# Head-mixing attention and two FFNs on one core: each batch's v load cut into eight DMAs, and a new listed order

## The chip, the core and the metric

The kernel runs on one core of a Trainium2 chip. The metric is the device time of one execution in microseconds (us). The profile tells the engines apart as PE (TensorE's matmuls), PEld (its weight loads), DVE (VectorE), ACT (ScalarE), POOL (GpSimd) and SP (SyncE, which issues most of the DMAs here). "Clock" is the share of TensorE's full speed that was granted in a stretch.

## The reference, cut to what matters

```python
def _attn_ref(q, k, v, w_pre, w_post):           # 4 batches, 12 heads, 448 rows, 64 columns
    scores = matmul(q, k^T) / sqrt(64)
    scores = einsum('bhij,hg->bgij', scores, w_pre)      # heads mixed before the softmax
    attn = softmax(scores)                               # over j
    attn = einsum('bhij,hg->bgij', attn, w_post)         # heads mixed after it
    return matmul(attn, v)

x = attn_out as (1792, 768)
x = (sigmoid(x @ w_gate) * (x @ w_val)) @ w_out          # 768 -> 1536 -> 768
h = x @ w_in                                             # 768 -> 2048
out = (h * sigmoid(1.702 * h)) @ w_out2                  # 2048 -> 768
```

All data are float32.

## The kernel before

The program has an attention part (the first 400 us) and the two feed-forward networks behind it, which this change leaves as they are.

In the attention a batch is cut into four units of 120 or 88 rows of q. For each unit PE first makes the scores of six pairs of heads (`qk`, L340), and DVE or ACT copy them from PSUM to the tile `sc` (`qk_out`). The unit is then taken in groups. For a group, SP moves rows of `sc` into a tile `gt` with two DMAs (`relayout`, L359) so that heads lie along the partitions; PE mixes the heads (`premix`, L368); DVE takes the maximum, ACT the exponential; PE mixes again (`postmix`, L415); DVE or ACT copy the result to the tile `at`. When all groups of a unit are done, PE multiplies `at` with v (`av`, L436). There are five `gt` tiles. Between these steps the q and k of the next batch are loaded into tiles `nat` (L291), turned on PE (`turn`, L300) and split in two parts, and 28 weight blocks of the first FFN are loaded (`pf`, L932), converted and stored again (`kept`, L898).

The tile `vt` holds the v of one batch; there is one such tile, so that a batch's v can be loaded only when the last `av` of the batch before has read it. `load_v` (L326) does it with two DMAs: x = 0 brings four of seven row groups into partitions 0 to 63, x = 1 the other three into partitions 64 to 127, each for all twelve heads. The first `av` of a batch needs both.

All of this is cut into pieces (`Work.add`), each with the engines that may run it. The order of all pieces on all engines, the engine of each piece and its PSUM banks stand in a table of numbers, `PLAN`, which `Work.order` reads: a token is the number of a piece in base 36, a letter for an engine where there is a choice, and banks behind a colon. The due times and costs in the calls of `work.add` are not used when the program is built. Every engine runs its own list in this order and waits for other engines by semaphores, so SP issues its DMAs strictly one after the other.

Of the kernel before, what the change touches and what calls it, by code (L numbers as in the profile page):

```python
# [74 lines left out]
0Y 3:0 1S 6:1 7V 1cY cS 1f:2 f:3 1oY 8 oS pS dY 4V 5 20:45 10S 11Y gV h r:6 sV 1gS 1h 1dS 1pS 2Y qY 21S u:7 vV  # L75
t i:1 eY jS k w 13:0 1r:3 16:2 14S 17V 22V 1i:6 1jS 23:41 1sS 1k 2c:75 15 25S 12S 24V 9:6 aS 18 2eS 1u:1 29:04
1t 1vV 1w 2dS 2bS 26:23 28S 1qY 2f:51 2aV 27V dd de 19:7 l:0 1x:4 2gS 2hV mV 1aV 1b b 4z:32 51V df:5 x:1 yV
1eS n dgV dh 1yS 1z 58:76 5aV 52:20 59S 54S 5e:75 2i 2j 2k:04 2l 53S 2v 50S di:2 2w 38 39 5gS 2n 3l 3m 3y 3z
4b 5fS z 2x:63 2y 2m 1l:5 1mV 1n 2z 2o 55:70 56S 4c 1fg 30 5b:15 5dV 3a:64 3b djS dk 31 32 2p 3c 3n:75 3d 3e
5cS 3f 2q 33 34 2r 57S 40:32 41 42 3o 3g 3h 3p 2s:64 3q 43 2tV 3r 3i:10 44 45 4d:37 4e 2uS 4g 4o 3jV 3kV 4f 4h  # L80
4i 4j 5h 7w:56 7yV 46 3s 5i 7xS 35:24 36S 3t 82:31 dl 7z:70 80V 37V 83S 84S 4k 88:56 89S 5u 85:23 87V 4l:17 3u
81V 3v:45 4mV 3wS 4nV 3xS 5j:30 47 48:17 5k 4p 5v 5m 86S 8b:45 49S 4aV 5l 5n 5w:21 4q:7 8cV 5x 5y 1fw 4r 67 68
5o 6k 5p 5q 8aV 4s dn:3 1fx 5z 60 69:40 4u:2 4v 6l 6x 6y 7a 7b 1fh 4w 8dV dt 5r:65 61 4tV 1fy 1fz 6a 8e 6b 6c
6d doS 6m:17 4xS dp 62 5sS 5tS 1g0 6z:40 7c:32 8f 8r 8s 6n 6p 6e 6o 6q 63 70 6f 71 72 73 1g2 at:65 avS auV
# [48 lines left out]
150:36 15d:71 15p 161 11rS 151 153 1jd 17cS 15e 122:05 123V 162 16e 124V 152 154 1jk 12f:24 12gS 12hS 1jj 14s
1jl 163:36 164 166 165 1jm 1jn 1jo 15q:05 14t 16f 17k 14u 15f 155 17l 156 1fs 15g 15r 17x 167 15t 157 12i:2
12j 12k 12m:4 12lS 12n 12o 12pV 15h 15i 16g:37 16h 15j 15s 15u 15k 16j 14v:62 16i 14wS 14xV 17m:10 17n 17y 18a
16k 17p 18b 158:45 15l:36 159V 15aV 17o 17q 16l 15mS 16m 168 169 16n 15v 19z:27 1ab:14 1adV 1a0S 16a 1acS
1a5:50 15nV 1a7V 1jq 1jr 1js 16o:32 16b:41 1jt 1ju 16cV 18c:60 1a6S 16pS 16r 1a1S 16dS 1a2:53 15w 1a3V 16qS
18n 1ae:71 18d 1agS 16s 18o 190 191 1a4S 1afV 18e 17r 1a8:42 1aaS 15x 1jp 18f 18g 1jw 15y:51 15zV 18p:37 18q
# [1635 lines left out]
```

## Time and profile before

| | |
|---|---|
| time, median of 3 runs | 1292.66 us (1284.29 to 1293.9) |
| profiled execution | 1287.18 us |
| its span | 1285.4 us |
| PE busy | 1247.9 us (97%) |
| DVE, ACT, POOL busy | 78%, 64%, 4% |

The span goes from the first to the last instruction of the profiled execution; the device time of the same execution lies 1.8 us above it. PE's busy time includes the time in which a matmul is only in flight, so 97% doesn't mean that PE works at its peak.

### The profile page before, as it was taken

The page shows a single profiled execution, that of the slowest core. Times are in us where ns is not written, and L with a number is a line of the kernel's source. Part 1 is how long each engine was busy: PE and PEld are TensorE (multiplying, and loading weights), DVE is VectorE, ACT ScalarE, POOL GpSimd, SP SyncE. Part 2 cuts the span into 40 slices and gives each one's busy share as a digit, 9 for nine tenths or more (in the row PEclk, how much of TensorE's full clock was granted, in tenths as well). Part 3 has the DMA queues.
Part 4 walks back from the last instruction along what each step waited for, and adds up shares of the span by engine and source line. Part 5 has one row for each costly group of instructions (what it writes and reads, how often), then busy time and mean ns, then how long its engine had stood idle before and what let it go on. Part 6 is the DMA issues. An engine that isn't in the chain of part 4 may idle for free.

```text
span 1285.4 us, 33205 instructions
## 1 busy us (share of the span) xinstructions
PE 1247.9 (97%) x12770; PEld 1115.6 (87%) x12770; DVE 1004.2 (78%) x2142; ACT 819.4 (64%) x1968; POOL 57.8 (4%) x138
## 2 busy tenths in 40 slices
PE   7999899899999999999999999999999999999998
PEld 5677676678679899989999999999999999999998
DVE  6787587698876999988889898878866795565863
ACT  3877587688884767667567666656665455565442
POOL 3111011010110000000000000000000000000000
PEclk9998899899999999999999999999999999999999
DMA  6877777677776665489976445894626872125653
GB/s 165 229 206 235 184 204 229 179 226 225 222 261 207 200 214 171 130 268 326 326 266 218 142 155 195 287 304 158 220 73 172 284 271 81 50 62 156 213 156 123
DMA packets 216111, 256.87 MB, mean 200 GB/s; under 512 B 60413, under 2 KB 202513, under 8 KB 215953
## 3 DMA queue, kind: packets, MB, share of 16 engines
q1 hardware_dynamic: 208944, 249.32, 61.7%
q0 software_dynamic: 1344, 4.05, 1.0%
q10 hardware_dynamic: 5664, 1.38, 0.5%
q8 instruction: 101, 1.65, 0.5%
q14 instruction: 58, 0.47, 0.1%
HBM read 160.18 MB, written 55.97 MB: 168 GB/s over the span
## 4 chain that ended last, share of the span: by engine, by line
PE 54%; DVE 7%; DMA 2%; issue 2%; ACT 1%; SPq 0%; DVEq 0%; ACTq 0%
PE pq L1155 27%; PE po L1642 14%; PE py L1100 13%; DVE xy L1137 1%; DVE w L1022 1%; DVE xy L1293 1%; DMA xy<-kept 1%; DVE s L1293 1%; DVE wc L894 1%; DMA sb<-xy 1%; DVE s L1164 0%; DMA wf<-sb 0%; ACT xy L1136 0%; DVE wt L1293 0%; DVE wc L893 0%
## 5 line engine op out<-in xcount | busy, mean ns | idle before, releaser
L1155 PE MATMUL pq<-xy,w 128*128 128x448 f32 x2394 | 482.1, 362 | 1.6 <-ACT s L1204 0.8
L1155 PEld LDWEIGHTS pq<-xy,w 128*128 128x128 f32 x2394 | 447.7, 187 | 35.3 <-ACT s L1204 2.3
L1642 PE MATMUL po<-wf,xy 128*128 128x384 f32 x1176 | 204.7, 335 | 2.6 <-DMA wf<-sb 2.6
L1642 PEld LDWEIGHTS po<-wf,xy 128*128 128x128 f32 x1176 | 203.9, 188 | 3.2 <-ACT xy L1088 2.3
L1100 PE MATMUL py<-xy,w 128*128 128x448 f32 x864 | 173.7, 362 | 1.5 <-DVE xy L1086 1.4
L1100 PEld LDWEIGHTS py<-xy,w 128*128 128x128 f32 x864 | 161.9, 187 | 12.9 <-DVE xy L1086 2.1
L380 ACT ACTIVATE ex<-bank,st 128x448 f32<-128x448 f32 x184 | 115.8, 635 | 29.3 <-DVE st L374 27.7
L415 PEld LDWEIGHTS bank<-w,ex 60*64 60x64 f32 (+1 forms) x5152 | 101.7, 136 | 35.3 <-issue 28.3
L374 DVE TENSOR_REDUCE st<-bank 128x1 f32<-128x448 f32 x184 | 107.3, 617 | 29.1 <-PE bank L368 25.8
L1136 ACT CAST xy<-xy 128x384 fp32r<-128x384 f32 (+2 forms) x212 | 89.1, 457 | 57.9 <-DVE xy L1293 55.0
L415 PE MATMUL bank<-w,ex 60*64 60x60 f32 (+2 forms) x5152 | 104.8, 222 | 11.4 <-issue 10.8
L1137 DVE TENSOR_TENSOR xy<-xy 128x384 fp32r<-128x384 f32 (+2 forms) x212 | 95.7, 486 | 22.4 <-ACT xy L1136 22.3
L1293 DVE TENSOR_TENSOR xy<-xy 128x384 f32<-128x384 f32 (+2 forms) x184 | 90.9, 512 | 15.8 <-DMA xy<-xd 7.0
L368 PE MATMUL bank<-gt,wpre 64*64 64x448 f32 (+2 forms) x736 | 96.3, 578 | 3.2 <-ACT at L304 2.9
L1016 ACT CAST w<-xy 128x384 fp32r<-128x384 f32 x110 | 55.1, 510 | 53.1 <-DVE xy L1293 29.2
L436 PEld LDWEIGHTS bank<-at,vt 128*64 128x64 f32 x1536 | 74.6, 138 | 14.2 <-ACT at L304 3.5
L340 PE MATMUL bank<-kq 64*120 64x448 f32 (+1 forms) x576 | 77.7, 396 | 6.1 <-issue 5.3
L1022 DVE TENSOR_TENSOR w<-wt,w 128x384 fp32r<-128x384 f32 x108 | 59.2, 553 | 27.6 <-ACT w L1016 27.6
L436 PE MATMUL bank<-at,vt 128*64 128x120 f32 (+1 forms) x1536 | 79.7, 262 | 0.7 <-ACT at L304 0.4
L890 ACT ACTIVATE wc<-ws 128x384 f32<-128x384 f32 x108 | 59.8, 554 | 30.1 <-DMA ws<-in_moe_w_in_dram 20.5
L340 PEld LDWEIGHTS bank<-kq 64*120 64x120 f32 (+1 forms) x576 | 52.5, 181 | 23.8 <-issue 7.1
L1164 DVE TENSOR_TENSOR s<-s,pq 128x448 f32<-128x448 f32 x80 | 49.4, 619 | 28.4 <-PE pq L1155 28.4
(98 smaller groups left out, 1534.6 us busy)
## 6 DMA issues: line engine op xcount, KB each, us to landing
gt<-sc SPq DMA_DIRECT2D x160, 210.0 KB
wf<-sb SPq DMA_DIRECT2D x64, 384.0 KB
xy<-kept SPq DMA_DIRECT2D x60, 384.0 KB
ws<-in_moe_w_out_dram SPq DMA_DIRECT2D x56, 384.0 KB
kept<-wc SPq DMA_DIRECT2D x108, 192.0 KB
ws<-kept SPq DMA_DIRECT2D x46, 384.0 KB
sb<-xy SPq DMA_DIRECT2D x32, 384.0 KB
ws<-in_moe_w_in_dram SPq DMA_DIRECT2D x32, 384.0 KB
```

The source lines that it names most:

```text
L340: nc.tensor.matmul(ps[a][:n, :S], w[at_, qp, 1, i0:i0 + n], w[at_, kp, 0], start=(i == 0), stop=(i == 2), tile_position=(a * 64, 0))
L368: nc.tensor.matmul(pre[s][row][64 * col:64 * col + 64, :S], wpre[r], x[r, col], start=True, stop=True, tile_position=(64 * row, 64 * col))
L374: nc.vector.tensor_reduce(out=rs[s][:, j:j + 1], in_=pre[s][j][:, :S], axis=AX.X, op=ALU.max, negate=True)
L380: nc.scalar.activation(ex[s][:, j], pre[s][j][:, :S], AF.Exp, bias=st[:, j:j + 1], scale=1.0, accum_out=st[:, 2 + j:3 + j])
L415: nc.tensor.matmul(ps[row][64 * k:64 * k + 64, c, :, j * m:(j + 1) * m], e[r, j, (c + k * NC) * 64:(c + k * NC + 1) * 64], w[r, j, :, i0:i ...
L436: nc.tensor.matmul(psv[u, half][a * 64:a * 64 + 64, r, :n], vt[:, g, c, :], at[:, c, g, :n], start=(c == 0), stop=(c == NC - 1), tile_posi ...
L1100: self.nc.tensor.matmul(acc[hb][:, :self.S], st, act[k0 + kc][hb][:, ap], start=(k0 + kc == 0 and part == 0 and ap == 0), stop=(k0 + kc == ...
L1136: self.nc.scalar.copy(dst[:, 0], src)
L1137: self.after(n, lambda: self.nc.vector.tensor_tensor(out=dst[:, 1], in0=src, in1=dst[:, 0].bitcast(F32), op=ALU.subtract))
L1155: nc.tensor.matmul(x, st, A[p][c][:, ap], start=(first and c + part + ap == 0), stop=(c == self.KG - 1 and part == 1), skip_group_check=no ...
L1293: self.nc.vector.tensor_tensor(out=dst, in0=x, in1=y, op=op)
L1642: nc.tensor.matmul(acc[:, :PW], x[:, part], w[:, wp], start=(start and part == 0 and wp == 0), stop=(stop and part == 1), skip_group_check ...
```

## The change

A batch's v comes in eight DMAs: for x = 0 and x = 1, four pieces of three heads each. Each piece is a piece of the plan with its own place in the table, and the first `av` of a batch needs all eight. The table is new as a whole: the pieces after the first v loads have other numbers, and the order of all pieces of the attention was searched again. Of the table two lines stand here.

```diff
 PLAN = """
-0Y 3:0 1S 6:1 7V 1cY cS 1f:2 f:3 1oY 8 oS pS dY 4V 5 20:45 10S 11Y gV h r:6 sV 1gS 1h 1dS 1pS 2Y qY 21S u:7 vV
...
+0Y 3:0 4V 1S 5 6:1 7V cY dS f:2 i:3 8 1cY 1f:4 20:56 oS r:7 1dY 1i:0 gV h pS 1gV 1h jS u:1 10Y 13:2 sV 21V 1oS
...
     EB = 5
+    VH = 3
     KB = NP + 2
...
-        def load_v(b, x):
+        def load_v(b, x, h0):

             c = slice(x * NC, min(x * NC + NC, HC))
-            nc.sync.dma_start(vt[64 * x:64 * x + 64, :, :c.stop - c.start],
-                              v[b].rearrange("h (m g) d -> m h g d", g=HC)[:, :, c])
+            h = slice(h0, h0 + VH)
+            nc.sync.dma_start(vt[64 * x:64 * x + 64, h, :c.stop - c.start],
+                              v[b, h].rearrange("h (m g) d -> m h g d", g=HC)[:, :, c])
...
-                                 lambda e, half=half, some=some: av(u, half, some), needs=[] if x else out[u] + [vready[b, c] for c in range(2)],
+                                 lambda e, half=half, some=some: av(u, half, some), needs=[] if x else out[u] + vready[b],
...
                 if ci == 0:
+                    vready[b] = []
                     for c in range(2):
-                        vready[b, c] = work.add((first[u] + 2 + 2 * c) * STEP + 1113, dict(SP=(800, 1000)), load=(2650, 2070)[c],
-                                                emit=lambda e, b=b, c=c: load_v(b, c), takes=("v",) if c == 0 else (),
-                                                behind=[vready[b, 0]] if c else [], since=0 if b else THIRD)
+                        for h0 in range(0, H, VH):
+                            vready[b].append(work.add((first[u] + 2 + 2 * c) * STEP + 1113 + 300 * h0, dict(SP=(650, 850)),
+                                                      load=(2650, 2070)[c] * VH // H,
+                                                      emit=lambda e, b=b, c=c, h0=h0: load_v(b, c, h0), takes=() if vready[b] else ("v",),
+                                                      behind=vready[b][-1:], since=0 if b else THIRD))
```

The first place is SP's list at the v load of the second batch (batch 1 of 0 to 3). Here and below `vt` is the v tile, `gt` a relayout, `pf` and `kept` the load and the store of a weight block, `nat` a load of q or k; `64x12x256` is partitions x heads x elements. Before:

```order
L359 DMA gt_278<-sc 120x1x448 x2
L359 DMA gt_279<-sc 120x1x448
L898 DMA kept_65<-pc 128x384
L932 DMA pf<-in_moe_w_val_dram 128x3x256
L359 DMA gt_279<-sc 120x1x448
L326 DMA vt<-in_v_dram 64x12x256
L326 DMA vt<-in_v_dram 64x12x192
L359 DMA gt_280<-sc 120x1x448
L291 DMA nat<-in_k_dram 112x4x64 x2
L359 DMA gt_280<-sc 120x1x448
```

The same place after:

```order
L362 DMA gt_278<-sc 120x1x448 x2
L362 DMA gt_279<-sc 120x1x448 x2
L938 DMA pf<-in_moe_w_val_dram 128x3x256
L329 DMA vt<-in_v_dram 64x3x256 x4
L329 DMA vt<-in_v_dram 64x3x192 x4
L362 DMA gt_280<-sc 120x1x448 x2
L904 DMA kept_65<-pc 128x384
```

Eight issues stand where two stood, next to each other; two loads of k that stood between the relayouts behind v are gone from here.

The second place is SP's list at the v load of batch 2. Before:

```order
L898 DMA kept_69<-pc 128x384
L359 DMA gt_280<-sc 120x1x448
L359 DMA gt_281<-sc 120x1x448 x2
L932 DMA pf<-in_moe_w_val_dram 128x3x256
L326 DMA vt<-in_v_dram 64x12x256
L326 DMA vt<-in_v_dram 64x12x192
L359 DMA gt_277<-sc 120x1x448
L898 DMA kept_69<-pc 128x384
L359 DMA gt_277<-sc 120x1x448
L932 DMA pf<-in_moe_w_val_dram 128x3x256
```

After:

```order
L362 DMA gt_277<-sc 120x1x448
L904 DMA kept_69<-pc 128x384
L938 DMA pf<-in_moe_w_val_dram 128x3x256
L329 DMA vt<-in_v_dram 64x3x256 x2
L362 DMA gt_277<-sc 120x1x448
L329 DMA vt<-in_v_dram 64x3x256 x2
L329 DMA vt<-in_v_dram 64x3x192 x4
L904 DMA kept_69<-pc 128x384
L938 DMA pf<-in_moe_w_val_dram 128x3x256
L362 DMA gt_278<-sc 120x1x448 x2
```

One relayout stands between the second and the third piece; the store and the load of weight blocks come right behind the last.

The third place is SP's list at the v load of batch 3. Before, one relayout stood between the two loads, and more behind them:

```order
L359 DMA gt_279<-sc 120x1x448 x2
L932 DMA pf<-in_moe_w_val_dram 128x3x256
L326 DMA vt<-in_v_dram 64x12x256
L359 DMA gt_280<-sc 120x1x448
L326 DMA vt<-in_v_dram 64x12x192
L359 DMA gt_280<-sc 120x1x448
L359 DMA gt_281<-sc 120x1x448 x2
```

After:

```order
L362 DMA gt_279<-sc 120x1x448 x2
L362 DMA gt_280<-sc 120x1x448 x2
L938 DMA pf<-in_moe_w_val_dram 128x3x256
L329 DMA vt<-in_v_dram 64x3x256 x4
L329 DMA vt<-in_v_dram 64x3x192 x4
L362 DMA gt_281<-sc 120x1x448 x2
```

The two relayouts of `gt_280` moved ahead of v, and all eight pieces stand together. In batch 0 the pieces stand apart: two among the first loads of q and k, six behind the first twelve relayouts and a weight load.

## Rows read from the trace of the kernel before

**Rows 1.** Page, part 1: busy time, share of the span, instructions.

```profile
PE 1247.9 (97%) x12770; PEld 1115.6 (87%) x12770; DVE 1004.2 (78%) x2142; ACT 819.4 (64%) x1968; POOL 57.8 (4%) x138
```

**Rows 2.** Stretches: start:end, length; busy us by engine; clock; DMA share; GB/s.

```profile
100.00:150.00 50.00, 43.26 (x991) 34.37 (x987) 34.41 (x75) 30.88 (x88) 5.04 (x12) 0.89 0.74 205
150.00:200.00 50.00, 49.91 (x1158) 38.51 (x1152) 42.69 (x90) 41.57 (x116) 6.63 (x15) 1.00 0.72 211
200.00:250.00 50.00, 43.47 (x1000) 33.64 (x998) 33.12 (x74) 32.64 (x92) 5.61 (x13) 0.90 0.72 207
...
0.00:400.00 400.00, 371.73 (x8253) 286.63 (x8254) 307.95 (x663) 295.11 (x807) 57.84 (x138) 0.97 0.74 213
400.00:1285.00 885.00, 876.16 (x4519) 828.99 (x4517) 696.28 (x1479) 524.31 (x1161) 0.00 (x0) 1.00 0.60 194
```

**Rows 3.** Waits of PE and PEld, 0 to 400 us: total us, times, longest.

```profile
PE bank L415 <- issue: 10.8, 8, 3.3
PE bank L340 <- issue: 5.3, 2, 4.6
...
PEld bank L368 <- issue: 7.7, 36, 0.3
...
PEld bank L368 <- DMA gt<-sc: 2.3, 7, 0.7
```

**Rows 4.** PE in order of time: start, us, what; in brackets the idle time before.

```profile
97.45 1.44 PE L368 MATMUL bank<-gt,wpre 64*64 64x448 f32 x4 [2.30 <-ACT at L304]
...
143.25 2.22 PE L340 MATMUL bank<-kq 64*120 64x448 f32 x10 [4.59 <-issue]
...
218.78 0.63 PE L415 MATMUL bank<-w,ex 48*64 48x48 f32 x27 [2.37 <-issue]
...
237.55 0.70 PE L415 MATMUL bank<-w,ex 60*64 60x60 f32 x17 [3.29 <-issue]
...
324.34 0.85 PE L415 MATMUL bank<-w,ex 60*64 60x60 f32 x38 [1.47 <-issue]
```

**Rows 5.** DMA queues: whole span; 133.2 to 140.1; 140.1 to 143.3; 227.0 to 234.7.

```profile
q8 instruction: 101, 1.65, 0.5%
...
DMA packets 1650, 1.43 MB, mean 207 GB/s; under 512 B 106, under 2 KB 1650, under 8 KB 1650
...
q1 hardware_dynamic: 1650, 1.43, 110.5%
...
q8 instruction: 1, 0.02, 3.2%
...
q1 hardware_dynamic: 1737, 1.60, 97.1%
```

**Rows 6.** SP's queue in order of time at the v loads: start, us of issue, what.

```profile
131.09 1.35 SPq L326 DMA_DIRECT2D vt<-in_v_dram  x2
...
226.45 1.39 SPq L326 DMA_DIRECT2D vt<-in_v_dram  x2
...
315.89 0.67 SPq L326 DMA_DIRECT2D vt<-in_v_dram  x1
...
236.26 0.39 SPq L932 DMA_DIRECT2D pf<-in_moe_w_val_dram  x1
```

**Rows 7.** Stretches of low and full clock; columns as in rows 2.

```profile
97.00:104.00 7.00, 6.55 (x84) 5.28 (x88) 4.02 (x7) 4.33 (x11) 0.00 (x0) 0.51 0.68 221
...
143.25:148.50 5.25, 5.25 (x52) 3.69 (x55) 2.59 (x6) 1.60 (x4) 0.39 (x1) 0.53 0.34 88
...
219.90:223.40 3.50, 3.50 (x34) 1.88 (x28) 1.95 (x5) 2.57 (x8) 0.38 (x1) 0.52 0.49 175
...
237.55:244.00 6.45, 6.45 (x99) 4.68 (x98) 1.85 (x3) 2.10 (x5) 0.00 (x0) 0.52 0.84 240
...
243.80:400.00 156.20, 151.81 (x3653) 120.72 (x3648) 128.73 (x274) 127.41 (x348) 19.67 (x45) 1.00 0.72 221
```

**Rows 8.** Waits of SP's queue, 0 to 400 us; columns as in rows 3.

```profile
SPq L932 <- DVE pc L896: 39.4, 20, 6.4
```

More of the change, by code (lines that the diff above doesn't have):

```diff
@@ L80 @@
[L80 to L84, printed above, removed]
@@ L135 @@
[L135 to L138, printed above, removed]
-160S 17z:62 106Y 18s 192:50 16t:1 1a9S 18r 18t 19d 18u 18v 19e 1ah 18h 18i 180 1ft 17s 17t 181 1jx 1ai 16u 182
@@ new lines @@
+4g 3i:21 3jS 4h 36V 37S 4i 3kV 45 4j 82:57 88:36 89V 8b:21 46 8aS 83S 3t 8e:40 8cV 84V 8gV 85:63 87V 1gl 86S
+8fS 4k 47 8h:52 1gm 4s 8dS 4t 4u 48:76 4l:04 4mS 8jS 49V 4aS 4nS 4v dt:3 duV 5n 5o 3u 60 61 6d 6e 6q 6r 73
+3v:17 3wS 1gn 3xS 5p:02 5q 62:64 8iS 5s 4w:1 4x 6f:75 dz 6g 74 5r 5t 5u 6i 5v 7g 7h 8k 8l 1go 4y 50:0 51 6h 52
+6j 63 65 dv 1g5 6s:27 64 6t 66 67 68 6k 5w 6v 4zS 6u 5x:56 5yS 75:34 5zV 76 69 6a:12 6bV 8x 8y 6l 6m 1gq e0
+az:56 78 6w 77 b1S 53V 6x 6y 7i:73 6n:16 7j 79 7l 8m:04 6oV 6cS 9a 9b b0S 7k 7m 7n 6z 6pV 7a 9n 70:25 7o 9o
@@ new lines @@
+13cV r4:5 r7:2 1hz n8 n9 obS mb 1hv o2S r8S ko:3 kp kq 1i0 lz m0 krS ks:7 oaV o3:01 mc r5V 13d r6 1i2 mp o5V
+rf:6 rk:4 ln rgV rh o4S 13j:3 rlS lo rj mq rm kt m1 ku kvS 13p oc od mr 13kV op r9 1i3 na:50 lp:16 lqS md 13l
+nb 1i4 m2:42 1i5 1i6 1i1 me nd oq p2 lrS m3V nc ms:73 mtS muV 1i8 mx:16 p3 ne m4S 1ga pf pg ps my mz 13e:5
+rn:4 n0 n1 roV 13fV nf rq:73 rrS rsS rt:02 rp rvS hzP ng n2 rw:16 ruS rz:74 rxV pt ryS n3 n4 s0V s5:32 s7S s1S
+s2:10 nh oe:67 1i9 s4S 13g s6V 13i s3V 1i7 mf:52 mgS 1ia ni:43 1ib 1ic 1ie mhV of oh 1id n5:10 njS nkS og s8
@@ new lines @@
+s9 n6S n7V kwP oi oj or:52 os ot ou ov ok ol ow p4:43 pu:61 pv px pw sl sm ph:07 p5 p7 p6 1if p8 13x ox 1ig
+1ih 1ii nl:5 nm sy nn np:2 noS nq 1ik nr p9 pi pk sz py pz q0 q1 oy pj pl pm sa:64 nsV om:35 q2:10 sb onS sd
+1gb pa tb ntP ooV tc 1ij uv:27 q3S uy:35 q4V sc se uzS sf uwV v4:10 va:62 vbS 1il v7:43 v9S v0V v6V v5V pb v8S
+v1:50 v3S vcS uxV to pn oz:16 p0S sn:73 p1S po 1im 1in 1io v2V so pp:40 pqV sp sq prV tp sr t0:52 t1 td:16
+pc:74 u1 u2 1gc pdS peV ss t2 te tg tq:03 q5:7 1iq q6 q7 t3 q9:4 vd ve qa qb 1ir 1is sg t4 1it tf st su q8V vq
@@ new lines @@
+10k:1 10l 12t 1k0 10jV 125 12d 12f 12u 10m 12e 155:46 11h:32 11t 126 10nV 12g 156 158 11u:07 11vV 11iS 11wV
+11jS 17q:51 12h 157 15t 182:32 183V 184V 17sS 17rS 1k2 1k3 1k4 1k1 17t:04 1k5 17uV 17vS 17w:71 127:53 17z:24
+17xS 128S 1k6 129V 12v 185:70 187V 17yS 15i:53 12w 12i 12j 180S 15u 166 167 16j 16k 16w 16x 181S 15v:12 186S
+15j 15l 12x:40 15k 15w 12yV 15m 12zV 12k:75 12lV 159 12mS 15a 15b 15n 15o 15x 168:34 169 16l:60 15c 1k8 1k9
+16m 16a 1k7 16b 15y 15z 15p 16n 160 1ka 1kb 130:5 131 132 1kc 16c 134:7 135 16o 188 133V 136 137S 16y:13
@@ new lines @@
+15d:26 16z 171 16p 161 16q 16r 15eS 15fV 162 170 189 18a:45 18b 18d 18l 18m 15q:70 18y 18z 19b 172 18c 15rV
+1gg 163:26 164V 18e 1an:13 18f 1apS 165V 1aw:74 1axV 1aoV 19c 173 1ke 179 17a 16s 174 17b 16d 17c 17d 17e 17f
+17g 16e 15sS 1kf 1kg 1kh 1az:52 1b0V 16f 18g 1b1S 1ayS 175 19o 1at:63 1auS 16t:07 16uS 1ki 19p 16vS 176:12
+190:46 1avS 191 193 1b2:50 177S 178S 192 1b4V 1b3V 1aq:73 194 18h 1asS 18n:12 16g:40 1arS 19d:65 19q:37 16hS
+16iV 195 19e 19f 17h:4 17i 19r 19s 19g 19t 1kk 1kd 1kl 1km 1kn 17j 196 19h 19u 19v 1ko 1a1 18o 17l:0 17m 18q
@@ new lines @@
+1bz 1co 1ky 1kz 1c1 1cq 1l0 1cp 1cr 1cg 1ahV 1cs 1gi 1ch 1c2 1aj 1ak 1alS 1c3 17pY 1c4 1d0:05 1d1 1bf:31
+1c5:47 1bgV 1bhS 1kv 1ef 1ct 1cu 1c6S 1d3 1eg 1c7V 1d2 1e4:21 1d4 1l2 1l3 1bs:63 1btV 1e5 1e6 1e7 1e8 1l4
+1ci:47 1cjS 1l5 1l6 1d5 1e9 1es 1buS 1ckS 1et 1f5 1ea 1f6 1d6 1eu:02 1ev 1ew 1ex 1l1 1ey 1cv:56 1cwS 1fi 1fj
+1gj 1eb 1eh:13 1ei 1l7 1ej 1cxV 1ek 1d7 1d8:47 1d9V 1f7:02 1f8 1daS 1l8 1l9 1lb 1db:1 1dc 1el 1em 1f9 1fa 1fb
+1ez 1f0 1fk:30 1fl 1la 1fn 1dd 1deV 1df:2 1fc 1en 1fm 1dg 1dh 1eo 1lc 1fo 1fp 1fq 1fr 1f1 1diV 1ma 1mb 1mc
@@ L154 @@
+1ec:31 1f2:02 1md 1edS 1lm 1eeS 1le 1fs:31 1ld 1mf 1ln 1f3S 1f4V 1lo 1mg 1ep:02 1ls 1lp 1lq 1lt 1lw 1lr 1n2
+1n3 1amY 1fd 1fe 1lu 1eqS 1erV 1mh 1ff:02 1ftV 1fuS 1lx 1mi 1lv 1n4 1lg 1mj 1ly 1m0 1fgS 1fhV 1mk 1mm 1lz 1m1
+1li 1m2 1m4 1mn 1fv:3 1fw 1fx 1lk 1m5 1m6 1m8 1m3 1n5 1n6 1m7 1lf 1lh 1m9 1n7 1mo 1mp 1mq 1fz:1 1mr 1mt 1mu
+1lj 1djP 1fyS 1mv 1mw 1mx 1g0 1ll 1g1 1ms 1my 1n0 1n1 1g2V 1g3 1n8 1n9 1na 1nb 1nc 1nd 1me 1ml 1mz
 """
```

113 lines of the change are left out of this document (45 added, 68 removed).

## The prediction

> **What bounds the kernel now.** I read first the page's shares: PE is busy for 97% of the span and every other engine for less [rows 1], so time can only come from what PE loses. The stages say where it loses: in the 400 us of attention 28.3 us of idle PE (400.00 less 371.73) and a mean clock of 0.97; in the 885 us behind it 8.8 us and a clock of 1.00 [rows 2]. The change touches the attention alone; what follows is the same program, which I take to move as a block.
>
> Inside the attention the loss is in few places. Two stretches of 50 us hold 13.3 us of idle PE, at a clock of 0.89 and 0.90; the one between them loses 0.1 us, at 1.00 [rows 2]. The list of waits gives the largest cause the name "issue", the PE waited for nothing that the profile shows: 10.8 us in the postmix (L415) and 5.3 us in the scores (L340) [rows 3]. The order of time shows them as gaps in the middle of a piece, where no buffer or semaphore is asked for: 4.59 us before 143.25, 3.29 before 237.55, 1.47 before 324.34; and 2.37 before 218.78 [rows 4].
>
> What those gaps wait for can be inferred from the DMA queues. PE ran 2 x 12770 instructions, and queue 8, marked "instruction", moved 101 packets: 253 PE instructions each [rows 1, 5]. So PE's own code comes through the same DMA engines, a packet about every 250 instructions. From 133.2 to 140.1 us queue 1 moved 1650 packets and queue 8 none; from 140.1 to 143.3 queue 8 moved one, and PE began again at 143.25 [rows 4, 5]. Likewise from 227.0 to 234.7: queue 1 alone, then one packet of queue 8, and PE at 237.55. And on SP's queue the two big v loads stand just ahead: at 131.09, at 226.45, and at 315.89, there with a relayout between the two [rows 6]. The code stood behind v, and PE ran dry. [...]
>
> **The change part by part.** *The v loads.* The bytes stay the same: 64 partitions x 12 heads x (256 + 192) elements of 4 bytes are 1.38 MB a batch, at the 207 GB/s that the queue moved there [rows 5] 6.6 us of all DMA engines. What changes is how fast they are put in line. Two issues took 1.35 to 1.39 us [rows 6], so the last byte stands 6.6 - 1.4 = 5.2 us deep when it is queued. The order shows the eight pieces next to each other on SP in three batches (one relayout between, in batch 2), so they are spread only by their own issue time. A piece has 3 x 64 runs. The trace has no such issue; the nearest rows are the weight load with 3 x 128 runs, 0.39 us, and the present v load with 12 x 64 runs, 0.67 to 0.70 us [rows 6]. I take 0.45, near the smaller, which has the next number of runs: 8 x 0.45 = 3.6 us, between 3.1 and 5.6. The line is then at most 6.6 - 3.6 = 3.0 us deep (1.0 to 3.5), 2.2 us less than now (1.7 to 4.2). A code packet that is asked for in that time comes so much earlier: the gaps of 4.59, 3.29 and 1.47 us become 2.4, 1.1 and 0. That is 2.2 + 2.2 + 1.5 = **5.9 us** (4.9 to 9.0 by the ends, and nothing if the packet's turn doesn't depend on the line). Batch 0's loads cost no visible gap now, and two of its pieces move ahead into the start; I cost them at nothing, with the first scores' loads as cover, and at the 2 pieces' 340 KB, 1.6 us at the same rate, if that cover is gone.
>
> [...]
>
> *The clock.* At half speed PE was busy throughout [rows 7], and loses at most the missing share of the clock: 5.25 x 0.47 = 2.5 us and 6.45 x 0.48 = 3.1 us. The clock also was low behind a gap of 2.37 us (0.52 in 219.9 to 223.4) and behind one of 2.30 (0.51 in 97 to 104), while behind the gap of 1.47 at 324 it stayed at 1.00 (from 243.8 on) [rows 4, 7]. The first gap's remainder of 2.4 us is like the former, the second's 1.1 like the latter. So I count the second stretch alone: **3.1 us** (0 to 5.6).
>
> *The order.* Counted in PE's order, changes between the forms of matmul (transposes, scores, the two mixes, attention times v) fall from 149 to 134. A change leaves PE's weight loads idle for 0.2 us where the profile names it (7.7 us in 36 times before L368 [rows 3]), but part of that lies under matmuls still running; per change 0 to 0.21 us, I take 0.1, so 15 x 0.1 = **1.5 us** (0 to 3.2). PE has the same pieces as before; seven copies out of PSUM go from DVE to ACT, neither of which is the bound [rows 1].
>
> *SP's queue.* Six more issues a batch, 3.6 - 1.4 = 2.2 us on SP, ahead of the relayouts (L359) on which each premix waits, and of the weight stores and loads. I cost this at nothing: the relayouts were queued behind v's bytes in any case, and SP itself stands waiting there for long (39.4 us for one vector step alone) [rows 8], while PE's weight loads waited for a relayout 2.3 us in all [rows 3]. Without that cover it is 3 x 2.2 = 6.6 us.
>
> *A new draw of the rest.* The gaps not next to a v load (2.30 and 2.37 us the largest [rows 4]) stood where code, stores and relayouts happened to meet in the old order. A new order will have its own, which can't be read from the order; I take the same sum, give or take 6 us.
>
> Sum: 5.9 + 3.1 + 1.5 = 10.5 us. The profiled execution took 1287.18 us, 1285.4 of them span, so 1276.7. The three runs have a median of 1292.66 and lie between 1284.29 and 1293.9; the four together have a mean of 1289.5, 2.3 above the profiled one, which I take as where the next median will lie. So **1279 us**.
>
> **The rivals.** *The line doesn't matter* (no change). The eight pieces stand together, the bytes are the same, and the code packet waits as long: because its turn doesn't depend on the line of queue 1, or because relayouts fill the place that v leaves. [...] For it: the gap at 218.78 has no v load near it [rows 4, 6]. Against: the three gaps with v hold 9.4 of the 16.1 us of "issue" [rows 3, 4]. Then only the 1.5 us remain: 1289.5 - 1.5 = 1288.
>
> *SP becomes late* (slower). Each relayout after the pieces leaves SP 2.2 us later, up to 5.6 - 1.4 = 4.2 us; the premix that waits for it stands ahead of everything on PE, so PE stands still so long in three batches, and the clock falls as after the gap of 2.37. Price: 3 x (4.2 + 2.8), with 2.8 the mean of the two clock losses above, 21 us: 1289.5 + 21, less the 1.5, 1309. It decides once relayouts land later than PE needs them, from which the 2.3 us of now are far. It would show as "PE L368 waits for DMA gt".
>
> *The new order clears the other gaps too* (faster). Then 2.30 + 2.37 = 4.7 us and the clock there, 7.0 x 0.49 + 3.5 x 0.48 = 5.1 us [rows 7], are saved as well: 1279 - 9.8 = 1269. For it: fewer changes of form and smaller loads everywhere; against: nothing in the change aims at those places.
>
> **How the numbers follow.** Chances: forecast 0.47, no matter 0.25, cleared 0.18, SP late 0.10. A measurement of this kernel can hardly tell less than 1% from nothing, 12.9 us. The bound of faster, 1279.7, runs through the forecast's middle: faster 0.47/2 + 0.17 = 0.40; slower, beyond 1305.6, 0.09; the rest 0.51. The range leaves out the slow rival and some of the tails: from 1266, which takes in the cleared case and the forecast with the upper ends of v and clock and a lucky draw (1279 - 3.1 - 2.5 - 6 = 1267), to 1295 (no saving at v, and 6 us of an unlucky draw on top of 1288).
>
> **What would show it.** Right: PE's "issue" waits in the attention fall from 16 us to 10 or less, the largest gap below 3 us, and queue 8 has a packet inside each stretch in which v is moved; the 50 us stretch around batch 2's v load has a clock of 1.00; eight v issues take 3 to 4.5 us on SP. Wrong: gaps of 3 to 5 us still stand behind the v loads; the eight issues take over 5 us; gaps with the name of a relayout, or of the v load before L436, which now lands later; or the clock is low over more than the four stretches of now.

## The result, and the profile after

The changed kernel takes 1279.74 us (median of 8 runs, 1274.46 to 1283.96), the kernel before 1291.62 (8 runs, 1284.29 to 1294.67): a ratio of 0.9897, with a 95% interval of 0.9871 to 0.9924. That is 11.9 us less. The profiled executions lie only 5.5 us apart, 1281.71 against 1287.18: that of after is 2.0 us over its median, that of before 4.4 us under its own. What the trace shows place by place is therefore read from one execution of each, and the size of each part is taken from the medians of the experiments.

Page of the changed kernel, part 1:

```profile
PE 1243.6 (97%) x12770; PEld 1112.2 (87%) x12770; DVE 998.1 (78%) x2134; ACT 822.6 (64%) x1976; POOL 58.5 (5%) x139
```

The same stretches as [rows 2], with the same columns:

```profile
100.00:150.00 50.00, 47.05 (x1134) 35.83 (x1128) 35.20 (x77) 38.78 (x109) 6.05 (x14) 1.00 0.83 230
150.00:200.00 50.00, 49.41 (x1106) 37.39 (x1103) 42.41 (x90) 41.75 (x115) 6.62 (x14) 1.00 0.78 221
200.00:250.00 50.00, 43.80 (x1170) 34.54 (x1168) 38.57 (x85) 36.60 (x104) 7.07 (x16) 1.00 0.82 220
0.00:400.00 400.00, 373.20 (x8293) 288.65 (x8294) 307.60 (x666) 299.62 (x817) 58.48 (x139) 0.99 0.76 219
400.00:1280.00 880.00, 870.41 (x4478) 823.50 (x4477) 690.49 (x1469) 523.01 (x1159) 0.00 (x0) 1.00 0.58 192
```

The two bad stretches of before had a clock of 0.89 and 0.90 and now have 1.00. The stretch around batch 2's v load still holds 6.2 us of idle PE.

Waits of PE, PEld and SP's queue in the first 400 us: total us, times, longest:

```profile
PE bank L418 <- issue: 8.8, 8, 2.6
...
PE bank L343 <- issue: 1.8, 1, 1.8
PE bank L439 <- issue: 1.3, 1, 1.3
PE bank L371 <- DMA gt<-sc: 1.2, 3, 0.5
...
PEld bank L371 <- issue: 7.3, 34, 0.4
...
PEld bank L371 <- DMA gt<-sc: 4.6, 6, 1.3
...
SPq L938 <- DVE pc L902: 24.5, 14, 5.3
```

In the two steps that stood at 10.8 and 5.3 us [rows 3], the postmix (now L418) and the scores (now L343), "issue" has fallen to 10.6. With every step of these 400 us it went from 16.5 to 14.7 only, since 1.3 us came in attention times v (L439) and 2.5 in the first FFN's matmuls (L1106). Idle PE fell from 28.3 to 26.8 us. The weight loads' waits for relayouts doubled, from 2.3 to 4.6 us, and SP stands 24.5 us for the vector step that took 39.4 [rows 3, 8]. PE in order of time, the gaps behind the v loads of batches 0, 1 and 2, and one behind none:

```profile
44.43 0.45 PE L418 MATMUL bank<-w,ex 60*64 60x60 f32 x9 [2.35 <-issue]
...
139.38 1.90 PE L343 MATMUL bank<-kq 64*120 64x448 f32 x16 [1.79 <-issue]
...
231.44 0.73 PE L418 MATMUL bank<-w,ex 60*64 60x60 f32 x29 [2.64 <-issue]
...
373.51 3.15 PE L1106 MATMUL pg<-xy,w 128*128 128x448 f32 x8 [2.46 <-issue]
```

Batch 1's gap of 4.59 us has become 1.79, batch 2's of 3.29 has become 2.64, and batch 3's of 1.47 is gone [rows 4]. The first and the last row are new places. SP's queue at the v loads of batches 1, 2 (behind its first two pieces) and 3, and all 32 v issues (ns: min/median/max):

```profile
130.68 7.22 SPq L329 DMA_DIRECT2D vt<-in_v_dram  x8
...
221.91 6.49 SPq L329 DMA_DIRECT2D vt<-in_v_dram  x6
...
305.45 7.61 SPq L329 DMA_DIRECT2D vt<-in_v_dram  x8
...
L329 SPq DMA_DIRECT2D vt<-in_v_dram x32: 595/610/1605, 11.1 to 312.5; - x32
```

Eight issues take 7 to 8 us where two took 1.35 to 1.39 [rows 6]: the median issue takes 0.61 us, but some take up to 1.6. DMA queues from 130.7 to 136.2, from 136.2 to 139.4, from 221.9 to 228.3, and from 228.3 to 231.4:

```profile
q1 hardware_dynamic: 1084, 1.15, 101.1%
q8 instruction: 1, 0.02, 1.1%
...
q1 hardware_dynamic: 785, 0.62, 108.0%
q8 instruction: 1, 0.02, 2.7%
...
q1 hardware_dynamic: 992, 0.99, 107.9%
...
q1 hardware_dynamic: 709, 0.58, 99.9%
q8 instruction: 1, 0.02, 3.3%
```

While v is put in line, a packet of code now gets through in batch 1; PE still ran dry there, and started again at 139.38 after the next one. In batch 2 a packet still comes behind 992 packets, and PE starts again at 231.44. The clock behind batch 0's gap, at the last gap, and behind batch 1's:

```profile
45.70:49.10 3.40, 3.40 (x22) 2.90 (x21) 2.18 (x7) 2.90 (x9) 1.12 (x3) 0.50 0.66 246
...
373.40:376.80 3.40, 3.29 (x16) 2.51 (x19) 0.41 (x1) 0.28 (x1) 0.00 (x0) 0.50 0.26 76
139.40:145.00 5.60, 5.60 (x138) 4.30 (x142) 2.19 (x5) 4.20 (x9) 0.59 (x1) 1.00 0.91 247
```

A clock of 0.50 is granted in two stretches of 3.4 us. Before, four stretches had 0.51 to 0.53, 22 us in all [rows 7].

### The profile page after: what moved, and what is told of

It is laid out like the page before. It is cut to its first block, busy times and chain, and to the rows that moved or that the text cites. A ratio compares the mean times of both kernels' runs of the same rounds, so it can differ in the third digit from the quotient of the medians.

```text
span 1280.0 us, 33240 instructions
## 1 busy us (share of the span) xinstructions
PE 1243.6 (97%) x12770; PEld 1112.2 (87%) x12770; DVE 998.1 (78%) x2134; ACT 822.6 (64%) x1976; POOL 58.5 (5%) x139
## 4 chain that ended last, share of the span: by engine, by line
PE 49%; DVE 7%; DMA 6%; ACT 2%; issue 2%; SPq 0%; DVEq 0%; ACTq 0%
PE pq L1161 27%; PE po L1648 16%; PE py L1106 6%; DMA ws<-in_moe_w_in_dram 3%; DMA sb<-xy 2%; DVE w L1028 1%; DVE xy L1143 1%; DVE s L1299 1%; DVE wc L900 1%; ACT ws L897 1%; ACT xy L1142 1%; DVE wc L902 1%; DVE s L1170 1%; DMA xy<-kept 0%; ACT w L1022 0%
## 5 line engine op out<-in xcount | busy, mean ns | idle before, releaser
L1106 PE MATMUL py<-xy,w 128*128 128x448 f32 x864 | 173.7, 362 | 1.4 <-DVE xy L1092 1.4
L1106 PEld LDWEIGHTS py<-xy,w 128*128 128x128 f32 x864 | 161.9, 187 | 12.9 <-DVE xy L1092 2.1
L418 PEld LDWEIGHTS bank<-w,ex 60*64 60x64 f32 (+1 forms) x5152 | 100.2, 134 | 34.9 <-issue 26.6
L418 PE MATMUL bank<-w,ex 60*64 60x60 f32 (+2 forms) x5152 | 104.1, 220 | 9.8 <-issue 8.8
L1143 DVE TENSOR_TENSOR xy<-xy 128x384 fp32r<-128x384 f32 (+2 forms) x212 | 95.5, 483 | 23.1 <-ACT xy L1142 22.7
L439 PEld LDWEIGHTS bank<-at,vt 128*64 128x64 f32 x1536 | 73.9, 137 | 14.0 <-ACT at L306 5.4
L439 PE MATMUL bank<-at,vt 128*64 128x120 f32 (+1 forms) x1536 | 78.7, 261 | 2.4 <-issue 1.3
L343 PE MATMUL bank<-kq 64*120 64x448 f32 (+1 forms) x576 | 73.9, 393 | 2.8 <-issue 1.8
L306 ACT COPY sc<-bank 120x448 f32<-120x448 f32 (+1 forms) x121 | 59.4, 546 | 19.0 <-DMA nat<-in_q_dram 9.0
```

Of the source, the lines that this page charges most:

```text
L343: nc.tensor.matmul(ps[a][:n, :S], w[at_, qp, 1, i0:i0 + n], w[at_, kp, 0], start=(i == 0), stop=(i == 2), tile_position=(a * 64, 0))
L418: nc.tensor.matmul(ps[row][64 * k:64 * k + 64, c, :, j * m:(j + 1) * m], e[r, j, (c + k * NC) * 64:(c + k * NC + 1) * 64], w[r, j, :, i0:i ...
L439: nc.tensor.matmul(psv[u, half][a * 64:a * 64 + 64, r, :n], vt[:, g, c, :], at[:, c, g, :n], start=(c == 0), stop=(c == NC - 1), tile_posi ...
L1106: self.nc.tensor.matmul(acc[hb][:, :self.S], st, act[k0 + kc][hb][:, ap], start=(k0 + kc == 0 and part == 0 and ap == 0), stop=(k0 + kc == ...
L1143: self.after(n, lambda: self.nc.vector.tensor_tensor(out=dst[:, 1], in0=src, in1=dst[:, 0].bitcast(F32), op=ALU.subtract))
```

## The experiments

All twelve, each against runs of the kernel before on the same chip. The ratio is not the quotient of the two medians (those of pool2 lie 3.2 us apart, its ratio makes 0.5 us):

| kernel | us, median | before | ratio, 95% |
|---|---|---|---|
| old8: old order, eight DMAs | 1282.0 | 1290.98 | 0.9928 (0.9899 to 0.9957) |
| new2: new order, two DMAs | 1288.82 | 1290.98 | 0.9973 (0.9947 to 1.0) |
| oldnone: old order, no v | 1275.75 | 1290.98 | 0.9881 (0.9848 to 0.9914) |
| newnone: new order, no v | 1269.58 | 1290.98 | 0.9837 (0.9806 to 0.9868) |
| spread0: batch 0's pieces apart | 1278.91 | 1292.23 | 0.9901 (0.9868 to 0.9934) |
| spread13: batches 1 and 3 apart | 1282.03 | 1292.23 | 0.9939 (0.9912 to 0.9965) |
| sp8: eight more issues on SP | 1285.99 | 1292.23 | 0.9956 (0.9932 to 0.998) |
| old24: old order, 24 DMAs | 1305.52 | 1292.23 | 1.0102 (1.0065 to 1.0139) |
| pool2: old order, two, by POOL | 1288.86 | 1292.08 | 0.9996 (0.9964 to 1.0028) |
| pool8: new order, eight, by POOL | 1280.73 | 1292.08 | 0.9921 (0.9893 to 0.9949) |
| new4: new order, four DMAs | 1284.72 | 1292.08 | 0.9961 (0.9928 to 0.9993) |
| shift128: old order, code shifted | 1297.65 | 1292.11 | 1.0059 (1.0026 to 1.0092) |

**The two parts of the change apart.** Theory A: PE's code waits behind v's bytes, so splitting gives the gain in either order. Theory B: the gain is the new order's. Four kernels cross the order with the form of v in batches 1 to 3; batch 0 keeps its own loads. The first splits v in the old order:

```diff
-            nc.sync.dma_start(vt[64 * x:64 * x + 64, :, :c.stop - c.start],
-                              v[b].rearrange("h (m g) d -> m h g d", g=HC)[:, :, c])
+            n = 3 if b else H
+            for h in range(0, H, n):
+                nc.sync.dma_start(vt[64 * x:64 * x + 64, h:h + n, :c.stop - c.start],
+                                  v[b, h:h + n].rearrange("h (m g) d -> m h g d", g=HC)[:, :, c])
```

> The old order, with each v load of batches 1 to 3 issued as four DMAs of three heads on the spot (batch 0 as before). Theory A (the code of PE waits in line behind v, and eight pieces make the line shorter): 4 to 9 us faster than before, the gaps behind v at most 3 us, the clock not low there twice. Theory B (the gain is the new order's): within 2 us of before, gaps of 3 to 5 us as before.

The second issues all twelve heads in the new order at the first piece of each half:

```diff
-            h = slice(h0, h0 + VH)
+            if b and h0:
+                return
+            h = slice(h0, h0 + (H if b else VH))
```

> The new order, with the v of batches 1 to 3 in two DMAs again, each issued where its first piece stands (batch 0 keeps its eight). Theory A: 4 to 9 us slower than the changed kernel, with gaps of 3 to 5 us behind v and a low clock after them. Theory B: within 2 us of the changed kernel.

The other two leave the v loads of batches 1 to 3 out (`if b: return` at the head of `load_v`), in the old and in the new order, so that these batches are multiplied with batch 0's v.

> The old order with the v loads of batches 1 to 3 left out, so that these batches are multiplied with the v of batch 0. It shows what these loads cost in all. Theory A: 12 to 17 us faster than before (gaps of 9 us and 5 to 6 us of clock gone). Theory B (v is hidden beside other work): at most 4 us.

> The new order with the v loads of batches 1 to 3 left out, so that these batches are multiplied with the v of batch 0. Theory A: 3 to 7 us faster than the changed kernel, the rest of the line of v. Theory B: about 0 to 2 us. Its distance from the old order without these loads is what the new order is worth by itself: 1.5 us by the changes of form, more if the other gaps went.

Splitting takes 9.0 us off in the old order (1290.98 to 1282.0) and 9.1 in the new one (1288.82 to 1279.74). The order gives 2.2 us with two DMAs (1290.98 to 1288.82) and 2.3 with eight (1282.0 to 1279.74), neither clear of the noise. So splitting gives the gain in either order, as A says, and B falls. The four kernels also price all of v: 15.2 us with two DMAs and 6.3 with eight in the old order, 19.2 and 10.2 in the new. The 10.2 is a miss of A, which expected 3 to 7; and without v the order gives 6.2 us (1275.75 to 1269.58), not 2.2. Such differences are uncertain by some 4 us each, so the parts add up for the splitting, and what the order is worth lies somewhere between nothing and these 6 us. PE in order of time in the new order with two DMAs, behind the v of batches 1, 2 and 3:

```profile
143.58 1.85 PE L345 MATMUL bank<-kq 64*120 64x448 f32 x8 [5.75 <-issue]
...
237.41 1.13 PE L420 MATMUL bank<-w,ex 60*64 60x60 f32 x28 [6.40 <-issue]
...
325.25 2.04 PE L420 MATMUL bank<-w,ex 60*64 60x60 f32 x63 [4.87 <-issue]
```

These are the gaps of before again, larger, in the other order. With eight DMAs in the old order no gap of 1.2 us or more stands behind v. PE's waits named "issue" in the postmix, first 400 us, of new2, old8 and oldnone:

```profile
PE bank L420 <- issue: 16.1, 8, 6.4
...
PE bank L417 <- issue: 10.0, 8, 3.0
...
PE bank L417 <- issue: 10.1, 8, 2.8
```

These are single executions: that of old8 is the fastest of its six, that of oldnone the slowest of its six.

**The pieces further apart.** The changed kernel, with the last three pieces of batch 0 behind later relayouts, and with those of batches 1 and 3 between the relayouts, stores and loads that follow (of batch 3: `17d 17e` behind `19o`, `17f 17g` behind `19p`, the weight load `1ke` behind `17b`):

```diff
-4s 8dS 4t 4u ... 4v dt:3 duV 5n 5o 3u 60 61 6d 6e
+4s 8dS ... dt:3 duV 5n 5o 4t 3u 60 61 4u 6d 6e 4v
```

> The changed kernel, with batch 0's last three v pieces moved behind the next three pairs of relayouts on SP, so that six issues no longer stand in a row there. Theory A (PE's code waits behind the bytes that SP has just put in line): in the changed kernel the six pieces at 36.2 to 40.2 us stand just ahead of a gap of 2.35 us in the postmix at 44.43 and of 3.4 us at half clock, 1.7 us lost: 4.0 us come back, and 1279.7 becomes 1276 (1274 to 1278), with no gap over 1.2 us between 40 and 50 us. Rival (the start's loss has another cause, such as the relayouts that queue there, or the gap moves to the next code packet): 1280, and a gap of 2 us or more stays between 40 and 60 us.

```diff
-hl hm hn ho hp l6:63 hq ... jy l2S h5S jz gq:50 l1S jn:16 1hj kb
+hl hm l6:63 ... jy hn l2S h5S jz ho gq:50 l1S jn:16 1hj hp kb hq
```

> The changed kernel, with the second half of v of batches 1 and 3 placed between the relayouts, the store and the weight load that follow, in place of eight in a row (batches 0 and 2 as they are). Theory A: the line of queue 1 is shorter still, batch 1's gap of 1.79 us goes and batch 3 stays without one: 1277 to 1279. The most that v can give back in all is 10 us, the 1279.7 against 1269.6 without those loads. Rival (what is left of v's cost is its bytes beside the relayouts, however they are spaced): 1280. Second rival (the first attention times v now waits for the last piece): a gap at L439 named DMA vt of 1 us or more in each of the two batches, 1282 to 1284.

Neither gave anything: 1278.91, not to be told from 1279.74, and 1282.03. In spread0's trace no gap over 1.2 us is left between 20 and 120 us, as expected. But the gap is not there in every execution either. Of the seven profiles with the changed kernel's batch 0, four have it (2.35, 2.10, 1.80 and 1.82 us) and three don't. In spread13 the place of batch 1's gap keeps 1.79 us, and no wait for v is named at attention times v, so neither its theory A nor its second rival shows in the trace. Setting the pieces further apart than SP's own pace does was a miss. The other v gaps are no more constant than batch 0's: spread0 leaves the pieces of batches 1 to 3 as the changed kernel has them, and from 123 to 364 us its trace has no gap of 1.2 us or more.

**SP's time.** Eight more small DMAs behind the last piece in the changed kernel:

```diff
+            if b and x and h0 == H - VH:
+                for n in range(8):
+                    nc.sync.dma_start(idle[:, n], v[b, n, :16, :16])
```

> The changed kernel, and behind the last v piece of batches 1 to 3 eight more DMAs of 16 runs of 64 bytes each, which move next to nothing but hold SP for some 3 to 5 us a batch, about as much as the six additional issues of the change did. It prices SP's time alone, the term that the prediction costed at nothing. Theory A (SP has that time, since it stands waiting for the vector engines and for free tiles anyway): 1279 to 1281, no new gap named DMA gt. Rival (SP becomes late): each relayout behind them comes that much later and PE stands: 3 x 3 to 5 us more, 1289 to 1295, with gaps named DMA gt at the premix.

And 24 DMAs of one head each in the old order (`n = 1 if b else H` in the loop of old8):

> The kernel before in its own order, with v of batches 1 to 3 in 24 DMAs of one head each on the spot, in place of two (batch 0 keeps its two). At 0.6 us an issue 24 take some 14 us for bytes that need 6.6, so that no line of v is left at all. Theory A (it is the depth of the line that PE's code waits for): no gap behind v, as little lost as with eight (1282.0) or less, down to the 1275.8 without v: 1278 to 1283. Rival (SP becomes late): 7 us more of SP a batch than with eight, of which PE stands still most: 3 x 7 = 21 us, 1300 or more, with gaps at the premix named DMA gt, or at attention times v named DMA vt.

The eight cost 6.25 us for the 17.8 us that they hold SP (5.11, 6.59 and 6.12), between the two expectations. In its trace the relayouts don't account for it: waits named DMA gt are 2.1 us on PE and 4.0 at its weight loads, against 1.2 and 4.6 in the changed kernel. Where these 6 us went is not shown.

```profile
PE bank L375 <- DMA gt<-sc: 2.1, 4, 1.0
...
PEld bank L375 <- DMA gt<-sc: 4.0, 5, 1.4
```

The 24 cost 23.5 us against eight: the rival's 1300 or more. Of the 24, SP's first batch and all issues (ns: min/median/max):

```profile
127.31 17.45 SPq L328 DMA_DIRECT2D vt<-in_v_dram  x24
...
L328 SPq DMA_DIRECT2D vt<-in_v_dram x74: 487/594/1567, 33.3 to 336.1; - x74
```

Waits of PE in the first 400 us of the same kernel, and its largest gap:

```profile
PE bank L370 <- DMA gt<-sc: 18.2, 8, 7.2
PE bank L417 <- issue: 7.1, 8, 1.5
...
PE bank L438 <- DMA vt<-in_v_dram: 2.7, 4, 1.1
...
246.91 1.76 PE L370 MATMUL bank<-gt,wpre 64*64 64x448 f32 x4 [7.16 <-DMA gt<-sc]
```

A piece a third as large takes as long to issue, 594 ns against 610. PE's "issue" is at its lowest of the old order's kernels, and the relayouts that SP could not issue took its place.

**Another queue, and four DMAs.** POOL in place of SP for batches 1 to 3, with two DMAs in the old order and with eight in the new:

```diff
-            nc.sync.dma_start(vt[64 * x:64 * x + 64, :, :c.stop - c.start],
+            (nc.gpsimd if b else nc.sync).dma_start(vt[64 * x:64 * x + 64, :, :c.stop - c.start],
```

> The kernel before in its own order, with the two v loads of batches 1 to 3 issued by POOL instead of SP: the same bytes in the same two DMAs, but in another queue than the relayouts and the rest. Theory A in the form that the bytes which wait in the DMA engines hold PE's code, whichever queue they came from: gaps of 3 us and more stay behind v in batches 1 and 2, and only the 4 us of SP time is saved: 1288 to 1291. Rival (it is the line within SP's queue that counts; queues take turns): the gaps behind v go, and the time is that of eight DMAs or less, 1276 to 1282. Third case (POOL stands waiting for the last attention times v with its multiplications for the postmix behind it): PE waits named POOL w, 1295 or more.

> The changed kernel, with the eight v pieces of batches 1 to 3 issued by POOL instead of SP. Eight additional small DMAs on SP (17.8 us of SP in all) cost 6.3 us, 0.35 us for each us of SP. The eight pieces hold SP for 21 us in all. Theory C (part of the gain of the eight pieces is paid back in SP's time): up to 21 x 0.35 = 7 us come back: 1273 to 1276. Rival (SP has time for eight, and only what comes on top of them is late): 1279 to 1281. Third case, as in the other kernel: POOL's multiplications for the postmix come late, 1284 or more, with PE waits named POOL w.

And four DMAs of six heads in the changed kernel:

```diff
-            h = slice(h0, h0 + VH)
+            if b and h0 % 6:
+                return
+            h = slice(h0, h0 + (6 if b else VH))
```

> The changed kernel with v of batches 1 to 3 in four DMAs of six heads, at the places of the first and third piece of each half (batch 0 as it is): half the issues, so some 3 us of SP a batch, and a line of 6.6 - 3 = 3.6 us. In this order two DMAs gave 1288.8 and eight 1279.7. Theory A alone (the line counts, 5.2 us deep with two and none with eight): 1288.8 - 9.1 x 1.6/5.2 = 1286 (1284 to 1287). Theory C (the line counts, and SP's time at 0.35 us for each us): four save 11 us of SP against eight, 4 us, so 1282, and if the two costs cross in between, 1278.

PE behind the v of batches 1 and 2 in pool2:

```profile
148.48 0.79 PE L415 MATMUL bank<-w,ex 60*64 60x60 f32 x15 [4.31 <-issue]
...
232.84 0.57 PE L415 MATMUL bank<-w,ex 60*64 60x60 f32 x19 [4.14 <-issue]
```

Its queues from 138.0 to 144.2, where PE stops, and from 144.2 to 148.5 (v is queue 0's):

```profile
q0 software_dynamic: 223, 0.86, 74.6%
q1 hardware_dynamic: 502, 0.21, 25.6%
...
q0 software_dynamic: 94, 0.39, 61.5%
q1 hardware_dynamic: 208, 0.25, 43.5%
q8 instruction: 1, 0.02, 2.2%
```

The gaps, 4.31 and 4.14 us, stay with v in another queue, so it is bytes in the DMA engines that the code waits for, not SP's queue. The time, 1288.86 us, lies where the first theory put it; the rival, with the gaps gone, expected 1276 to 1282. Queues 0 and 1 moved side by side here. But from 138.0 until PE ran dry at 144.2, 725 packets of theirs passed and none of queue 8, and its one packet came in the 4.3 us behind. The packets of such counts are not alike: they hold 0.87 KB each in queue 1 of before, about one run of v [rows 5], and 3.9 KB in queue 0 here. When the code was asked for is not among these rows, so they agree with a long wait without showing how long it was.

pool8 (1280.73) gained nothing from the 22.7 us that v held SP in the changed kernel. That agrees with SP having had that time for eight pieces, but doesn't show it: in pool8 v came later, and PE stood 2.64 us for it.

```profile
149.59 2.72 PE L439 MATMUL bank<-at,vt 128*64 128x120 f32 x26 [2.64 <-DMA vt<-in_v_dram]
```

new4 (1284.72) is where A alone put it, but theory C's 1282 is within its uncertainty too. In the new order two, four and eight DMAs make 1288.8, 1284.7 and 1279.7. None of these kernels separates how deep the line is from how large each DMA in it is: splitting makes both smaller, and setting small pieces further apart gained nothing.

**Is it code?** That "issue" means PE's own code was inferred from 253 instructions a packet (2 x 12770 to 101 packets of queue 8 [rows 1, 5]). The kernel before, with 128 more PE instructions at the start, and no DMA changed:

```diff
+            for _ in range(64 if (b, p, i) == (0, 0, 0) else 0):
+                nc.tensor.transpose(pst[b, p, i][:16, :16], ident[:16, :16], ident[:16, :16])
```

> The kernel before, with 64 small transposes (128 PE instructions, matmul and weight load counted apart) ahead of the first real one, at a place where PE still waits for its first data; all DMAs and their order stay. It tests whether the gaps named issue are PE's own code coming late. If PE's code comes in packets of some 253 instructions (theory A), the gaps stand at fixed counts of instructions since the start, so that everything is cut 128 instructions earlier in the program. In the two kernels so far gaps stood after 4969 and 4962 (PE and PEld together), 8255 and 8241, 9015 and 9002 instructions. With the additional 128 counted, a gap then stands within 20 of 4965 or 5220 for batch 1 and within 20 of 8750 or 9010 for batch 2, and not where the old places of the program would be, at 5097 and 9143. The packet behind batch 1's v was asked for soon behind the two issues; one asked for 3 us earlier is ahead of them, and the next finds half of the line gone: the gap of 4.59 us falls to 2 us or less. In batch 2 the packet falls nearer to the issues and the gap of 3.29 us stays or grows, up to 6 us. Time within 5 us of before, 1286 to 1296. Rival (something at these places of the program, a bank or a wait that the profile doesn't show): gaps at 5097 and 9143, 4.6 and 3.3 us, and the time of before.

Stretches of the kernel before that end inside its gaps at 143.25, 237.55 and 324.34; the counts of the first two engines are PE's and PEld's:

```profile
0.00:143.20 143.20, 125.92 (x2484) 93.15 (x2485) 105.70 (x231) 94.51 (x257) 25.53 (x65) 0.97 0.77 207
...
0.00:237.50 237.50, 213.66 (x4507) 161.23 (x4508) 177.45 (x387) 165.80 (x455) 38.16 (x93) 0.96 0.75 206
0.00:324.30 324.30, 298.71 (x6531) 227.53 (x6531) 250.08 (x541) 234.30 (x647) 48.52 (x117) 0.96 0.74 208
```

The same of shift128, inside its gaps of 3.28, 1.27, 1.97 and 4.19 us:

```profile
0.00:142.70 142.70, 127.81 (x2611) 94.33 (x2612) 108.04 (x237) 95.87 (x261) 26.00 (x66) 0.99 0.78 207
0.00:226.10 226.10, 209.15 (x4508) 157.84 (x4508) 175.50 (x384) 163.03 (x449) 38.26 (x93) 0.98 0.78 212
0.00:231.80 231.80, 212.89 (x4635) 160.98 (x4635) 178.32 (x389) 166.80 (x458) 38.26 (x93) 0.99 0.78 212
0.00:312.90 312.90, 289.36 (x6531) 220.38 (x6532) 247.12 (x535) 231.29 (x639) 48.22 (x116) 0.99 0.78 215
```

The sums are 4969, 9015 and 13062 before; 5223, 9016, 9270 and 13063 with the shift. The gaps stand at the same counts from the start, or 254 more, although every step of the program comes 128 later in the count: what PE lacks is cut by its instruction count and not by the step of the work. That is code, and shown. The sizes went only in part as expected. Batch 1's gap became 3.28 us, not 2 or less; batch 2's two make 3.2, at the low end. Batch 3's, not expected, grew from 1.47 to 4.19, and two more came away from v, 2.70 us before 41.64 and 2.82 before 377.56. The time came out 5.5 us above before by the medians, beyond the 5 us that were allowed; the profiled execution, 1288.36 us, is the fastest of the seven, so what made that up beside these gaps was not separated.

## Why the prediction was right

**The sum.** The forecast was 1279, the measured median 1279.74. Two errors offset each other in it: the saving was put at 10.5 us and measured 11.9, and the median of before at 1289.5, where eight runs give 1291.62. The prediction's v loads and clock, 5.9 and 3.1, make 9.0; splitting alone measured 9.0 and 9.1. Its order term of 1.5 measured 2.2 and 2.3; the part of it that the profile names, the weight loads' "issue" at the premix, went from 7.7 us in 36 times to 7.3 in 34. The experiments that confirm this were each uncertain by some 4 us, so the agreement to a few tenths is luck.

**The v loads, by place.** Predicted were gaps of 2.4, 1.1 and 0 us; the profile has 1.79, 2.64 and 0, 4.9 us less than before. The way there was off in one step: an issue was taken at 0.45 us. The median issue takes 0.61, and eight take 7 to 8, longer than the 6.6 us that their bytes need at the 207 GB/s of [rows 5], so by the prediction's own formula no line of v is left and the gaps should have gone altogether. In spread0's execution and in old8's they did; in this one they did not. Even without v the old order has 10.1 us of "issue" in the postmix, no less than with eight DMAs (10.0), so code is late where no v is moved too. The formula saw v alone.

**The clock.** Only the second stretch was counted, 3.1 us. In the profile both, with 0.53 and 0.52 before [rows 7], are gone, 2.5 and 3.1: the upper end, 5.6. The two low stretches away from v went too, 5.1 us by the prediction's price, and the two new ones cost at most 1.7 us each. So in this pair of profiles the clock makes more of the difference than the 1.5 us by which idle PE fell. The reading by the length of a gap (low behind 2.4 us, full behind 1.1) did not hold: the clock stayed at 1.00 behind batch 2's gap of 2.64 us and fell to 0.50 behind batch 0's of 2.35. Why is open.

**SP's queue.** Costed at nothing, and pool8 agrees with that. But the cover ends soon: 17.8 us more of SP cost 6.25 us, and 24 pieces hold SP 32 us longer than eight (old8's issues take 19.8 in all, old24's 52.2) and cost 23.5. The rival "SP becomes late" had the right mechanism and the right sign in its waits (DMA gt), at three times the number of pieces.

**Batch 0.** Costed at nothing. In the profile it lost 2.35 us and half the clock for 3.4 us, 4.0 in all, which no row of before announced. In other executions the gap is not there, and taking it away saved nothing that could be measured. The term is mis-sized for this profile and small on average. The fallback's 340 KB were too few: the two pieces that moved to the start are both of the larger kind, 64 x 3 x 256 elements, 393 KB together.

**The new draw.** The gaps at 97.45 and 218.78 went [rows 4], others came at 213.16 (1.62), 219.25 (1.33) and 373.51 (2.46). So the rival in which the order clears the other gaps did not come about; "about the same sum" did.

**The signs.** Of those that were to show it right, the clock of 1.00 around batch 2's v load and a largest "issue" gap below 3 us came true. "Issue" came to 10.6 us in the two steps that were counted, not 10 or less; queue 8 had no packet between 221.9 and 228.3; and eight issues took 7 to 8 us, over the 5 that stood among the signs of being wrong. The time came out right with that step wrong.

**The line doesn't matter.** This rival falls with the two splits. The form of it in which the code packet's turn doesn't depend on queue 1's line, so that the size of a load can't matter, falls with new2, new4 and the changed kernel (1288.82, 1284.72 and 1279.74 us), which differ in the number of pieces.

What stays open: whether the code waits for the whole line or for the DMA that is being moved, and why eight pieces still cost 10.2 us in the new order and 6.3 in the old one. Spacing them further and taking them off SP did not get it back, and the two differences are within each other's uncertainty.

## What to carry to other kernels

When PE idles in the middle of an unrolled loop and the profile names "issue", count its instructions up to the gap. Here gaps stood whole packets of 253 to 254 instructions apart, code was late, and the large transfer queued just ahead was what to cut. It paid, with 9.0 and 9.1 us, to cut it until the issues (7 to 8 us) took about as long as the bytes need (6.6 us). Far beyond that it didn't: 24 pieces kept SP for 17 to 18 us in a batch, and what stood behind them in its queue came late. Between eight and 24 nothing was measured. A gain of this kind is made of a few stalls that not every execution has, so size it by medians of both parts apart, not by one pair of profiles.

## What was not expected of the hardware

The packets can be counted: gaps of the changed kernel stand at 8241, 8495 and 9002 instructions (PE and PEld together), 254 and 2 x 253.5 apart. Over the whole program it is 2 x 12770 instructions to 101 packets, 253 each. At one such count, 4969 in the kernel before, PE stood still for 4.59 us [rows 4].

A DMA with a third of the runs took SP as long to issue: 594 ns in the median for 64 runs of a head, 610 for three heads, and the eight tiny DMAs of 16 runs still 418.
